# Fused attention and two MLP layers on one core: attention's instructions in an order computed in the source, fixed tiles, pair 0 loaded head by head

## The chip, the cores and the metric

The kernel runs on one core of a Trainium2 chip. The metric is device time in microseconds (us) of one execution, the median of the runs shown; lower is better. The core's engines run their own instruction queues in order: PE (TensorE, matmuls and transposes), DVE (VectorE), ACT (ScalarE), POOL (GpSimd) and SP (SyncE, which here only issues transfers).

## The reference

Attention with rotary embedding on q and k, then two MLP layers on the attention's output:

```python
q, k, v: (2, 8, 576, 64); tokens 2*576 = 1152; d_model 512; d_ff 1536 and 2048
q_rot, k_rot = rotate(q), rotate(k)
scores = matmul(q_rot, k_rot.T) / sqrt(64)
attn = exp(scores - max(scores)); attn = attn / (sum(attn) + 1e-9)
x = (attn @ v) as (1152, 512)
x = ((x @ w_a) * (x @ w_b)) @ w_out
h = x @ w_in;  out = (h - tanh(h)) @ w_out2
```

## The kernel before

**Precision.** Every operand of a real matmul is split into a high part (a rounded fp32r copy) and a low part (the remainder), so each product is made of two or three fp32r matmuls. A split costs a copy on ACT (the high part) and a subtraction on DVE or POOL (the low part). The weights come as 64-bit floats and are converted on ACT and DVE in pieces (`conv_unit`, L116) that are issued between other work.

**Attention by pairs of heads.** There are 2 batches with 8 heads: 8 pairs of heads, run one after the other as a software pipeline. For each pair:

- loads of q and k (`load_qk`, L237) and of v (`load_v`, L245), all on SP's queue; the rotary embedding (`rope_step`, L264), four instructions for q and four for k: on DVE for pair 1, on POOL from pair 2; the split of v (`prep_v`, L282: ACT, then POOL);
- `prep_T` (L342): PE transposes (L363), ACT makes the high part `th` (L366), DVE the low part (L368), and eight transfers on SP move them to `q2` and `k2` (L383);
- nine score units (`s_unit`, L387): 40 matmuls of 288 columns a pair (L409) into one of two score tiles in PSUM (tag `s`), the row maximum on DVE (L415), the exponential with the row sum on ACT (`s_exp`, L421). A score tile is free again after its exponential;
- the probabilities are transposed on PE (`t_unit`, L474; `t_tail`, L455, L460, L461: 42 transposes a pair) into three PSUM tiles of tag `t`, which `prep_T` and the normalization use too, and split by ACT (L479, L446) and DVE (L481, L448);
- `v_head` (L484): 40 matmuls (L501) into the accumulator; ACT copies it to `xe` (L523), a transfer moves one half to the other partitions of `xsum` (L525), and POOL adds the halves (L526). Pair 7 does this with ACT and DVE alone (L517, L519);
- `norm_sum` (L531) and `norm_pair` (L548): the reciprocal of the sums on DVE, spread by POOL into `rd` (L541, L545), transposed by PE (L554, L555: five), multiplied into `xsum` by DVE (L557, L560); then the output's high part by DVE (L562) and low part by POOL (L563).

Pair 0 is different: one transfer brings both heads of q or k per half of the partitions, and `rope_head` and `prep_head` (L299, L314) prepare it head by head on DVE, PE (L324) and ACT without transfers.

**What sets the order.** A loop over "slots" calls these functions at places that a table of offsets fixes (`at(...)`, L589 on; the offsets in `CFG`), and the framework's scheduler then reorders the instructions of each engine by its own estimates and by the priorities `P_...` in `CFG`. Tiles come from rotating pools. The result is a static order per engine. In the last pair the first pieces of weight conversion and the first matmuls of the next stage (`ab`, L190) are mixed in.

**After attention** come the matmuls of the two MLP layers (`ab`, `y`, `h`, `o`), with the weights' conversion between them. The change does not touch these functions.

Of the kernel before, what the change touches and what calls it, by code (L numbers as in the profile page):

```python
CFG = {'EXPF': 1, 'MAXF': 1, 'TT0': 20, 'TT1': 17.5, 'NS': 19, 'NP': 31, 'LK': -8, 'LQ': -2, 'RK': -2, 'RQ': 1, 'PK': 2, 'PQ': 4.5, 'LV': 7, 'PV': 9, 'WC1': 6, 'WC2': 4, 'PST': 3, 'RE': 2, 'FST': 0, 'CY': 1, 'CA': 2, 'CH': 2, 'OE': 3, 'VA0': 5.5, 'VA1': 7, 'VB0': 0, 'VB1': 2, 'PKD': 1, 'PQD': 0, 'PVD': 2, 'PVE': 0, 'XHE': 2, 'RST': 0, 'PA': 99, 'PB': 0, 'PO': 4, 'YLP': 4, 'GA': 0, 'GB': 0, 'WF': 99, 'WCE': 5, 'NH': 2, 'HA': 0, 'NT2': 2, 'RB': -50, 'SB': -49, 'NW': 20, 'NW1': 6, 'TM': 1, 'CO': 1, 'CHB': 0, 'WG': 99, 'WCG': 4, 'TL': 7, 'P_pl': 0, 'P_norm_sum': 30, 'P_load_v': 0, 'P_prep_v': 30, 'P_pT': 60, 'P_tl': -15, 'XL': 7, 'RDP': 1, 'P_ph': 0, 'P_exp': -60, 'P_V': 0, 'P_rope_head1': 0, 'P_load_qk': 15, 'P_S': 0, 'P_xs': -15, 'P_T': 0}
# [10 lines left out]
F32 = mybir.dt.float32  # L12
# [13 lines left out]
C2 = 0.052115944387372236  # L26


@with_exitstack
def attention_moe_kernel(  # L30
# [13 lines left out]
    nc = tc.nc  # L44
# [171 lines left out]
    with ExitStack() as actx:  # L216
        ap1 = actx.enter_context(tc.tile_pool(name="ap1", bufs=1))
        ap2 = actx.enter_context(tc.tile_pool(name="ap2", bufs=2))
        sctx = ExitStack()
        ps_s = sctx.enter_context(  # L220
            tc.tile_pool(name="ps_s", bufs=2, space=bass.MemoryType.PSUM, side="right")
        )
        ps_t = actx.enter_context(tc.tile_pool(name="ps_t", bufs=PST, space=bass.MemoryType.PSUM, side="left"))
        ps_v = actx.enter_context(tc.tile_pool(name="ps_v", bufs=4-PST, space=bass.MemoryType.PSUM, side="left"))

        rtab = ap1.tile([P, 2, 5 * D], F32, name="rtab")
        zero = ap1.tile([P, 2 * D], F32, name="zero")
        raw = [ap1.tile([P, 2, 5, D], F32, name=f"raw{n}") for n in "qk"]
        q2 = []
        for i in range(2):  # L230
            t = mid.tile([P, 2, 2, 640], F32R, tag="mid", name=f"q2{i}")
            q2.append(t)
        v2 = [ap1.tile([P, 10, 2 * D], F32R, name=f"v2{i}") for i in range(2)]

        def halves(t, b, hp):
            return t[b, 2 * hp:2 * hp + 2].rearrange("h (r c) d -> r h c d", c=CW)

        def load_qk(i, n):
            b, hp = PAIRS[i]
            s = halves((q, k)[n], b, hp)  # L240
            t = raw[n]
            nc.sync.dma_start(out=t[0:64], in_=s[:, :, 0:5])
            nc.sync.dma_start(out=t[64:128, :, 0:4], in_=s[:, :, 5:9])

        def load_v(i):  # L245
            b, hp = PAIRS[i]
            vr = ap1.tile([P, 2, CM, D], F32, tag="vr", name="vr")
            vt = ap1.tile([P, D], F32, tag="vt", name="vt")
            s = halves(v, b, hp)
            nc.sync.dma_start(out=vr[0:64], in_=s[:, :, 0:4])  # L250
            nc.sync.dma_start(out=vr[64:128], in_=s[:, :, 5:9])
            vf = v[b, 2 * hp:2 * hp + 2].rearrange("h (r c) d -> (h r) c d", c=CW)
            nc.sync.dma_start(out=vt, in_=vf[:, 4])
            vraw[i] = (vr, vt)

        vraw = {}
        k2 = {}
        pt = {}
        sums = {}
# [3 lines left out]
        rtmp = {}  # L263
        rot = {}  # L264

        def rope_step(n, step, eng):
            t = raw[n].rearrange("p h c d -> p c h d")
            if step == 0:
                rtmp[n] = ap1.tile([P, 5, 2, D], F32, tag=f"r2{n}", name="r2")
                rot[n] = ap1.tile([P, 5, 2, D], F32, tag=f"ro{n}", name="ro")  # L270
            if step < 2:
                o0, o1 = step * hd, (1 - step) * hd
                eng.tensor_tensor(
                    out=rtmp[n][:, :, :, o0:o0 + hd], in0=t[:, :, :, o1:o1 + hd],
                    in1=sb[:, :, :, o0:o0 + hd].to_broadcast([P, 5, 2, hd]), op=ALU.mult,
                )
            elif step == 2:
                eng.tensor_tensor(out=rot[n], in0=t, in1=cb.to_broadcast([P, 5, 2, D]), op=ALU.mult)
            else:
                eng.tensor_tensor(out=rot[n], in0=rot[n], in1=rtmp[n], op=ALU.add)  # L280

        def prep_v(i, h):  # L282
            vr, vt = vraw[i]
            v2i = v2[i % 2]
            cp = (nc.scalar.copy, nc.gpsimd.tensor_copy, nc.vector.tensor_copy)[PVE]
            if h < 2:
                dst = v2i[:, 4 * h:4 * h + 4, :]
                hi, lo = (dst[:, :, D * x:D * x + D] for x in (h, 1 - h))
                cp(out=hi, in_=vr[:, h])
                nc.gpsimd.tensor_tensor(out=lo, in0=vr[:, h], in1=hi, op=ALU.subtract)  # L290
                return
# [54 lines left out]
        def prep_T(i, n, h):  # L346
# [25 lines left out]
            if h == 0:  # L372
                return
# [531 lines left out]
```

## Time and profile before

| what | value |
|---|---|
| three runs | 625.51, 624.96, 621.99 us; median 624.96 us |
| the profiled execution | 619.34 us, its span 617.6 us |
| PE busy | 587.5 us (95% of the span) |
| DVE, ACT, POOL busy | 486.0 us (79%), 347.8 us (56%), 133.1 us (22%) |
| stretch of attention | from about 17 us (first score matmul) to about 192 us |

The profiled execution is 5.6 us below the median of the runs. The page gives busy times and what bounded the end; windows give busy time by stretch, the timeline single instructions with what they waited for, and the chain of waits the work that released each next step. Matmuls are pipelined, so that a busy PE is not yet a PE at its best rate.

### The profile page before, as it was taken

How to read it: one execution, taken by the hardware profiler on the slowest of the kernel's cores; microseconds unless marked ns; L12 is line 12 of the kernel's file. 1: busy time of each engine (PE TensorE's matmuls, PEld its weight loads, DVE VectorE, ACT ScalarE, POOL GpSimd, SP SyncE). 2: the span in 40 equal slices, each digit the busy share in tenths (PEclk: the TensorE clock that was granted, in tenths of full speed). 3: DMA queues.
4: the chain of work that ended last, by engine and by line, in shares of the span. 5: the costliest groups of instructions: out<-in, count | busy, mean ns of one | idle time of the engine just before them, and what ended most of it. 6: DMA issues, size and time to landing. Idle time of an engine off the chain costs nothing.

```text
span 617.6 us, 9091 instructions
## 1 busy us (share of the span) xinstructions
PE 587.5 (95%) x3468; PEld 551.8 (89%) x3468; DVE 486.0 (79%) x654; ACT 347.8 (56%) x579; POOL 133.1 (22%) x137
## 2 busy tenths in 40 slices
PE   7699998799989999999999999999999999999997
PEld 6588997788879999999999999989988988998975
DVE  7988888778888989787747468798976797899572
ACT  2588887688864566434223233358775773575350
POOL 2758888863320000000000000190000000000000
PEclk9999999999999999999999999999999999999999
DMA  4565765456243555424212123320001122300014
GB/s 118 144 155 138 187 153 142 125 137 140 79 146 109 187 183 174 167 70 136 69 59 78 69 69 137 119 86 1 1 24 45 69 69 68 115 22 1 1 41 112
DMA packets 37771, 60.91 MB, mean 99 GB/s; under 512 B 4064, under 2 KB 22496, under 8 KB 37728
## 3 DMA queue, kind: packets, MB, share of 16 engines
q1 hardware_dynamic: 37728, 60.34, 33.6%
q8 instruction: 27, 0.44, 0.3%
q14 instruction: 16, 0.13, 0.1%
HBM read 43.06 MB, written 2.36 MB: 74 GB/s over the span
## 4 chain that ended last, share of the span: by engine, by line
PE 72%; DVE 10%; ACT 8%; POOL 3%; DMA 3%; issue 2%; SPq 0%; POOLq 0%; ACTq 0%; DVEq 0%
PE ab L190 23%; PE h L190 11%; PE o L828 11%; PE y L190 9%; PE pss L409 5%; PE acc L501 5%; PE pst L474 4%; PE ow L828 3%; POOL yt L721 2%; ACT p L421 2%; ACT ph L479 2%; PE psp L363 1%; ACT st L127 1%; POOL xsum L526 1%; DMA st<-in_moe_w_in_dram 1%
## 5 line engine op out<-in xcount | busy, mean ns | idle before, releaser
L190 PE MATMUL ab<-xt,w 128*128 128x384 f32 x504 | 89.2, 335 | 1.3 <-DVE xsum L557 0.8
L190 PEld LDWEIGHTS ab<-xt,w 128*128 128x128 f32 x504 | 87.3, 188 | 1.8 <-issue 1.1
L828 PE MATMUL o<-wc,g 128*128 128x512 f32 x348 | 83.7, 392 | 0.5 <-ACT g L803 0.4
L828 PEld LDWEIGHTS o<-wc,g 128*128 128x128 f32 x348 | 64.7, 188 | 14.1 <-ACT g L803 1.4
L190 PE MATMUL y<-g,wc 128*128 128x384 f32 x432 | 76.5, 334 | 0.0
L190 PEld LDWEIGHTS y<-g,wc 128*128 128x128 f32 x432 | 75.0, 188 | 0.0
L409 PE MATMUL pss<-k,q 128*128 128x288 f32 x320 | 62.4, 315 | 6.6 <-ACT p L421 4.5
L190 PE MATMUL h<-yt,w 128*128 128x384 f32 x360 | 65.5, 335 | 0.0
L190 PEld LDWEIGHTS h<-yt,w 128*128 128x128 f32 x360 | 62.9, 188 | 1.7 <-issue 0.4
L190 PE MATMUL ab<-xt,wc 128*128 128x384 f32 x360 | 63.2, 334 | 0.0
L190 PEld LDWEIGHTS ab<-xt,wc 128*128 128x128 f32 x360 | 62.5, 188 | 0.0
L415 DVE TENSOR_REDUCE nm<-pss 128x1 f32<-128x576 f32 x72 | 53.5, 752 | 11.2 <-PE pss L409 10.9
L721 POOL TENSOR_TENSOR yt<-yacc,yt 128x384 fp32r<-128x384 f32 x12 | 17.6, 1497 | 206.1 <-ACT yt L720 206.1
L501 PE MATMUL acc<-ph,v 128*128 128x288 f32 x320 | 56.8, 307 | 3.5 <-ACT ph L479 2.6
L127 ACT ACTIVATE st<-st 128x1024 f32<-128x1024 f32 x34 | 39.8, 1170 | 35.4 <-DMA st<-in_moe_w_b_dram 16.4
L421 ACT ACTIVATE p<-pss,nm 128x576 f32<-128x576 f32 x72 | 54.1, 752 | 7.2 <-DVE nm L415 6.9
L409 PEld LDWEIGHTS pss<-k,q 128*128 128x128 f32 x320 | 45.8, 189 | 11.9 <-ACT p L421 9.0
L688 ACT COPY tmpa<-ab 128x384 f32<-128x384 f32 x36 | 17.2, 477 | 60.7 <-PE ab L190 60.6
L474 PE MATMUL pst<-ident,p 128*128 128x128 f32 x288 | 45.2, 274 | 5.6 <-DVE xsum L557 2.3
L481 DVE TENSOR_TENSOR ph<-pst,ph 128x512 fp32r<-128x512 f32 x72 | 48.2, 684 | 2.6 <-ACT ph L479 2.2
L501 PEld LDWEIGHTS acc<-ph,v 128*128 128x128 f32 x320 | 45.5, 188 | 5.3 <-ACT ph L479 1.6
L479 ACT CAST ph<-pst 128x512 fp32r<-128x512 f32 x72 | 42.0, 594 | 12.2 <-PE pst L474 11.4
(120 smaller groups left out, 984.6 us busy)
## 6 DMA issues: line engine op xcount, KB each, us to landing
st<-in_moe_w_out_dram SPq DMA_DIRECT2D x14, 1024.0 KB, 4.8
st<-in_moe_w_in_dram SPq DMA_DIRECT2D x8, 1024.0 KB, 5.1
q<-th SPq DMA_DIRECT2D x28, 288.0 KB, 5.1
st<-in_moe_w_a_dram SPq DMA_DIRECT2D x12, 512.0 KB, 3.6
st<-in_moe_w_b_dram SPq DMA_DIRECT2D x12, 512.0 KB, 4.8
k<-th SPq DMA_DIRECT2D x28, 160.0 KB, 2.7
vr<-in_v_dram SPq DMA_DIRECT2D x16, 128.0 KB, 2.9
out_dram<-oacc SPq DMA_DIRECT2D x16, 128.0 KB, 2.4
```

The lines of the kernel that those rows point to most:

```text
L127: nc.scalar.activation(out=xs.bitcast(F32), in_=xs.bitcast(F32), func=AF.Copy, scale=2.0 ** -112)
L190: nc.tensor.matmul(ps, w(a), x(c), start=start and n == 0, stop=stop and n == 2)
L409: nc.tensor.matmul(ph[:, a], st, k2[i][:, j, ko + a * HS:ko + (a + 1) * HS], start=(n == 0), stop=(n == len(mms) - 1),)
L415: nc.vector.tensor_reduce(out=nm[:, u:u + 1], in_=ph, axis=AX.XY, op=ALU.max, negate=True)
L421: nc.scalar.activation(out=po.rearrange("p (a x) -> p a x", a=2), in_=ph, func=AF.Exp, bias=nm, scale=1.0, accum_out=sm,)
L474: nc.tensor.transpose(ps[:, t * P:(t + 1) * P], p[:, t, o:o + P], ident)
L479: nc.scalar.copy(out=pu[:, 0, qm(i)], in_=ps)
L481: nc.vector.tensor_tensor(out=pu[:, 1, qm(i)], in0=ps, in1=pu[:, 0, qm(i)], op=ALU.subtract)
L501: nc.tensor.matmul(acc, st, pslot(i, u)[:, s, a * HS:(a + 1) * HS], start=(u == 8 and s == 0), stop=(u == full[-1] and s == 1),)
L688: nc.scalar.copy(out=a[:, t], in_=r[0])
L721: (nc.gpsimd if YLP > d else nc.vector).tensor_tensor(out=yl, in0=o, in1=yh, op=ALU.subtract)
L828: nc.tensor.matmul(ps, g[:, a, i * P:(i + 1) * P], wc[:, c, f % 2], start=(n == 0 and m == 0), stop=(n == GE - 1 and m == 2),)
```

## The change

- `make_ops` lists every instruction group of the attention (some 90 a pair) with its engine, its duration, what it reads and writes, and its PSUM tile. `plan` places them in time, engine by engine, by these durations and by a rank (`OFF`, one number per kind, found beforehand). The groups are emitted in the order of the planned starts, and up to the last exponential the framework keeps that order on all five queues (`tc.manual_schedule`). The rest of pairs 6 and 7 is emitted in the planned order too, with a piece of weight conversion each 1.3 us of planned time, and there the framework may still reorder. The priorities are gone.
- The tiles are fixed ones (two `k2`, two `p`, one `xe`, one `xsum`, and so on) in place of pools that rotate. The PSUM pools stay: three tiles of tag `t`, two of `s`, one accumulator.
- Pair 0's q and k come in eight transfers, one per head and half of the partitions: four issued by ACT at its start, four by SP; q's first head is prepared first.
- The embedding of pair 1 moves from DVE to POOL. The output's high part moves from DVE (L562) to ACT, its low part from POOL (L563) to DVE.

```diff
+def make_ops(NPR, XL):
...
+            op(i, f"S{u}", "PE", c * .132, (c - 1) * .132 + .33, r=kq, w=[g], g=g, args=(i, u))
+            op(i, f"max{u}", "DVE", .668, .76, r=[g], w=[("nm", b, u)], g=g, args=(i, u))
+            op(i, f"exp{u}", "ACT", .735, .76, r=[g, ("nm", b, u)], w=[pb + (u,), ("sm", b, u)], g=g, args=(i, u))
...
+        op(i, "xh", "ACT", .55, .65, r=xk, w=[("xh", i)], args=(i,))
+        op(i, "xl", "DVE", .67, .75, r=xk + [("xh", i)], w=[("xl", i)], args=(i,))
+    return ops
...
+def plan(ops, off, noise=None, look=0.0, start=None):
+    n = len(ops)
+    rank = [o[0] * II + off.get(o[1], 0.0) + off.get((o[1], o[7]), 0.0) for o in ops]
...
+START = {'DVE': 5.2, 'PE': 6.0, 'SP': 3.3, 'ACT': 3.0, 'POOL': 12.0}
+OFF = {
+    'S0': -25.13, 'S1': -41.8, 'S2': 6.72, 'S3': 0.3, 'S4': 4.19, 'S5': 10.11, 'S6': 14.05, 'S7': 8.11, 'S8': 2.6,
...
-                    eng = nc.vector if j < RE else nc.gpsimd
-                    at(g0 + LK, load_qk, j, 1)
-                    at(g0 + LQ, load_qk, j, 0)
...
-            (nc.scalar.copy, nc.gpsimd.tensor_copy, nc.vector.tensor_copy)[XHE](out=xh, in_=x)
-            nc.gpsimd.tensor_tensor(out=xl, in0=x, in1=xh, op=ALU.subtract)
...
+        def x_hi(_, i):
+            nc.scalar.copy(out=x_out(i)[0], in_=x)
+
+        def x_lo(_, i):
+            xh, xl = x_out(i)
+            nc.vector.tensor_tensor(out=xl, in0=x, in1=xh, op=ALU.subtract)
...
+        for j in range(2):
+            for n in (1, 0):
+                s = halves((q, k)[n], 0)
+                nc.scalar.dma_start(out=raw[n][0:64, j], in_=s[:, j, 0:5])
+                nc.sync.dma_start(out=raw[n][64:128, j, 0:4], in_=s[:, j, 5:9])
...
+        ops = make_ops(NPR, XL)
+        begin = plan(ops, OFF, start=START)[0]
+        todo = sorted(range(len(ops)), key=lambda n: begin[n])
+        scored = max(n for n, o in enumerate(todo) if ops[o][:2] in ([NPR - 1, f"exp{u}"] for u in range(9))) + 1
...
+        with tc.manual_schedule(engines=set(engines)):
+            for o in todo[:scored]:
+                emit[ops[o][1]](ops[o][6], *ops[o][7])
...
+        last = begin[todo[scored]]
+        for o in todo[scored:]:
+            while begin[o] > last + CVT:
+                cv(1)
+                last += CVT
+            emit[ops[o][1]](ops[o][6], *ops[o][7])
```

How the order moves, at three places. In the rows, `pss` is a score tile, `psp` the transposes of q or k, `pst` those of the probabilities, `acc` the accumulator, `ro` or `rot` the embedded q or k, `r` or `rtmp` its partial products.

PE in the fill of the pipeline, from the first score matmul of pair 0; before:

```order
L409 MATMUL pss<-k_145,q_93 128x288 x12
L363 MATMUL psp<-ident,ro 128x128 x6
L409 MATMUL pss<-k_145,q_93 128x288 x16
L363 MATMUL psp<-ident,ro 128x128 x6
L460 MATMUL pst<-ident,p_241 128x128
L461 MATMUL pst<-ident,p_241 64x128
L409 MATMUL pss<-k_145,q_93 128x288 x4
L474 MATMUL pst<-ident,p 128x128 x4
L409 MATMUL pss<-k_145,q_93 128x288 x4
L474 MATMUL pst<-ident,p 128x128 x8
L409 MATMUL pss<-k_145,q_93 128x288 x4
```

With the change:

```order
L649 MATMUL pss<-k_98,q_96 128x288 x8
L584 MATMUL pss<-ident,rotk 128x64
L584 MATMUL pss<-ident,rotk 128x128 x4
L767 MATMUL warm<-ident 128x128 x6
L649 MATMUL pss<-k_98,q_96 128x288 x20
L671 MATMUL pst_321<-ident,p_104 128x128 x4
L671 MATMUL pst_327<-ident,p_104 128x128 x4
L671 MATMUL pst_334<-ident,p_104 128x128 x4
L649 MATMUL pss<-k_98,q_96 128x288 x8
L541 MATMUL psp_357<-ident,rotq 128x128 x4
L541 MATMUL psp_366<-ident,rotq 128x128 x2
L649 MATMUL pss<-k_98,q_96 128x288 x4
```

Score matmuls now start before k's second head is transposed (`rotk` after the first eight), pair 0's scores and the transposes of its probabilities run on without the transposes of pair 1 between them (`psp` came after 12 score matmuls, now after 36 and 12 transposes).

POOL around the end of a pair in the middle of the attention (`xsum<-xe` adds the halves, `rd<-rs` spreads the reciprocals, `v` is the split of v); before:

```order
L526 TENSOR_TENSOR xsum<-xe,xsum 64x576
L541 COPY rd<-rs 128x512
L545 COPY rd<-rs 128x128
L526 TENSOR_TENSOR xsum<-xe,xsum 64x576
L273 TENSOR_TENSOR r_1497<-rawk,rtab 128x10x32 x2
L273 TENSOR_TENSOR r_1585<-rawq,rtab 128x10x32
L278 TENSOR_TENSOR ro<-rawk,rtab 128x640
L563 TENSOR_TENSOR xt_73<-xsum,xt_72 128x576
L280 TENSOR_TENSOR ro<-ro,r_1497 128x640
L273 TENSOR_TENSOR r_1585<-rawq,rtab 128x10x32
L278 TENSOR_TENSOR ro<-rawq,rtab 128x640
L280 TENSOR_TENSOR ro<-ro,r_1585 128x640
```

With the change:

```order
L736 COPY rd<-rs_112 128x512
L740 COPY rd<-rs_112 128x128
L635 TENSOR_TENSOR v_100<-vr,v_100 128x4x64
L533 TENSOR_TENSOR rotq<-rotq,rtmpq 128x640
L526 TENSOR_TENSOR rtmpk<-rawk,rtab 128x10x32 x2
L526 TENSOR_TENSOR rtmpq<-rawq,rtab 128x10x32
L719 TENSOR_TENSOR xsum<-xe,xsum 64x576
L635 TENSOR_TENSOR v_100<-vr,v_100 128x4x64
L719 TENSOR_TENSOR xsum<-xe,xsum 64x576
L635 TENSOR_TENSOR v_100<-vt,v_100 64x64 x2
L526 TENSOR_TENSOR rtmpq<-rawq,rtab 128x10x32
```

The two additions stood on either side of the spreading; now both come behind it, with parts of later pairs' embedding and of v between them, and the output's low part (`xt`) is gone from POOL.

DVE at the same place (`nm` is the row maximum, `xsum<-xsum` the normalization, `xt` the output); before:

```order
L415 TENSOR_REDUCE nm<-pss 128x1 x2
L560 TENSOR_TENSOR xsum<-xsum,rt 64x64
L557 TENSOR_TENSOR xsum<-xsum,rb 128x512
L560 TENSOR_TENSOR xsum<-xsum,rt 64x64
L415 TENSOR_REDUCE nm<-pss 128x1
L562 CAST xt_72<-xsum 128x576
L368 SCALAR_TENSOR_TENSOR th<-psp,th 128x448
L481 TENSOR_TENSOR ph<-pst,ph 128x512
L368 SCALAR_TENSOR_TENSOR th<-psp,th 128x192
L415 TENSOR_REDUCE nm<-pss 128x1
```

With the change:

```order
L678 TENSOR_TENSOR ph_116<-pst_1619,ph_116 128x512
L655 TENSOR_REDUCE nm_109<-pss 128x1
L747 TENSOR_TENSOR xsum<-xsum,psrb 128x512
L751 TENSOR_TENSOR xsum<-xsum,psrt 64x64 x2
L655 TENSOR_REDUCE nm_109<-pss 128x1
L678 TENSOR_TENSOR ph_115<-pst_1663,ph_115 128x512
L655 TENSOR_REDUCE nm_108<-pss 128x1
L678 TENSOR_TENSOR ph_115<-pst_1683,ph_115 128x512
L762 TENSOR_TENSOR xt_73<-xsum,xt_72 128x576
L655 TENSOR_REDUCE nm_108<-pss 128x1
```

The output's cast, which followed one maximum after the normalization, is replaced by the low part's subtraction, which stands two maxima and two splits (`ph`) behind the normalization.

## Rows read from the trace of the kernel before

**Rows 1.** The page, part 2: the granted TensorE clock in 40 slices.

```profile
PEclk9999999999999999999999999999999999999999
```

**Rows 2.** Windows: stretch, length, busy us (instructions) of PE, PEld, DVE, ACT, POOL; clock; DMA.

```profile
17.11:35.74 18.63, 13.32 (x88) 10.22 (x86) 17.47 (x30) 13.24 (x35) 15.52 (x16) 1.00 0.64 160
35.74:168.81 133.07, 122.48 (x926) 114.70 (x926) 110.04 (x203) 107.86 (x278) 91.22 (x95) 1.00 0.56 138
55.00:115.00 60.00, 54.99 (x424) 52.03 (x422) 50.56 (x97) 49.85 (x129) 52.14 (x54) 1.00 0.64 157
55.00:155.00 100.00, 90.31 (x693) 85.07 (x691) 82.44 (x156) 80.91 (x210) 74.27 (x78) 1.00 0.60 145
168.81:191.80 22.99, 20.16 (x136) 18.40 (x135) 21.07 (x35) 12.50 (x23) 3.69 (x4) 1.00 0.42 137
```

**Rows 3.** Timeline of PE: start us, us, line, op, out<-in, count [idle before <-releaser].

```profile
17.11 0.38 PE L409 MATMUL pss<-k,q 128*128 128x288 f32 x1
...
35.74 0.51 PE L409 MATMUL pss<-k,q 128*128 128x288 f32 x2
...
54.95 0.38 PE L554 MATMUL rb<-ident,rd 128*128 128x128 f32 x2
...
155.10 0.38 PE L554 MATMUL rb<-ident,rd 128*128 128x128 f32 x2
```

**Rows 4.** Chain of waits, stretches of PE alone: start us, us, what.

```profile
66.90 1.32 PE acc L501 x10
...
68.66 0.53 PE pss L409 x4
69.20 0.44 PE pst L474 x4
...
191.80 8.21 PE ab L190 x46
```

**Rows 5.** Waits of PE, 55 to 155 us: total us, times, longest.

```profile
PE pst L474 <- DVE xsum L557: 2.3, 2, 1.3
PE pst L474 <- DVE th L368: 1.6, 2, 1.0
...
PE psp L363 <- DVE xsum L560: 0.7, 1, 0.7
```

**Rows 6.** Chain of waits at one end of a pair.

```profile
112.75 1.35 POOL xsum L526
...
116.79 1.44 POOL xsum L526
...
118.25 0.69 DVE xsum L557
...
120.02 1.78 DVE xt L562
```

**Rows 7.** Timeline of DVE at the start.

```profile
2.27 0.20 DVE L580 CAST q<-zero 128x64 fp32r<-128x64 f32 x1 [0.75 <-ACT zero L575]
...
6.17 0.56 DVE L304 TENSOR_TENSOR r<-rawk,rtab 128x160 f32<-128x160 f32 x2 [2.06 <-DMA rawk<-in_k_dram]
```

**Rows 8.** Chain of waits in pair 0's scores.

```profile
23.70 0.68 DVE nm L415
...
24.40 0.84 ACT p L421 x2
```

**Rows 9.** Timeline of DVE, two instructions of one form beside POOL and without it.

```profile
8.26 1.02 DVE L308 TENSOR_TENSOR r<-rawq,rtab 128x320 f32<-128x320 f32 x1
...
11.19 0.48 DVE L308 TENSOR_TENSOR r<-rawk,rtab 128x320 f32<-128x320 f32 x1
```

**Rows 10.** One line's instructions: duration ns min/median/max, first and last start.

```profile
L562 DVE CAST xt<-xsum x8: 450/460/1785, 59.7 to 191.7; 128x576 fp32r<-128x576 f32 x8
```

**Rows 11.** Waits of SP's queue, 55 to 155 us.

```profile
SPq L525 <- ACT xe L523: 14.4, 3, 10.4
```

**Rows 12.** The page, part 6: transfers, count, KB each, median us to landing.

```profile
q<-th SPq DMA_DIRECT2D x28, 288.0 KB, 5.1
```

More of the change, by code (lines that the diff above doesn't have):

```diff
@@ L235, in halves @@
[L235 to L254, printed above, removed]
@@ new lines, in v_hi, with v_lo, s_ph, s_mm @@
+        def v_hi(_, i, h, j):
+            dst, src = v_part(i, h, j, 0)
+            nc.scalar.copy(out=dst, in_=src)
+        def v_lo(_, i, h, j):
+            dst, src = v_part(i, h, j, 1)
+            nc.gpsimd.tensor_tensor(out=dst, in0=src, in1=v_part(i, h, j, 0)[0], op=ALU.subtract)
+        def s_ph(g):
+            return tile_of(g).rearrange("p (a x) -> p a x", a=2)[:, :, 0:HS]
+        def s_mm(g, i, u):
+            mms = []
+            for j in ((0, 1) if u == 8 else (u // 4,)):
+                for s in range(2):
+                    o, ko = (SM * (1 - j), 64) if u == 8 else ((u % 4 + j) * P, 64 * (1 - j))
+                    mms.append((q2[i % 2][:, s, j, o:o + P], j, ko))
+            for m, (st, j, ko) in enumerate(mms):
+                for a in range(2):
+                    nc.tensor.matmul(
+                        s_ph(g)[:, a], st, k2[i % 2][:, j, ko + a * HS:ko + (a + 1) * HS],
+                        start=(m == 0), stop=(m == len(mms) - 1),
+                    )
@@ new lines, in t_mm, with t_hi, t_lo, tail_T @@
+        def t_mm(g, i, u):
+            o = SM if u == 8 else u * P + (u // 4) * P
+            for t in range(CM):
+                nc.tensor.transpose(tile_of(g)[:, t * P:(t + 1) * P], pt[i % 2][:, t, o:o + P], ident)
+        def t_hi(g, i, u):
+            nc.scalar.copy(out=pslot(i, u)[:, 0, qm(i)], in_=tile_of(g))
+        def t_lo(g, i, u):
+            dst = pslot(i, u)
+            nc.vector.tensor_tensor(out=dst[:, 1, qm(i)], in0=tile_of(g), in1=dst[:, 0, qm(i)], op=ALU.subtract)
+        def tail_T(g, i, part):
+            t, p = tile_of(g), p8[i % 2]
@@ new lines, in v_mm, with x_copy, x_move @@
+        def v_mm(g, i, j, a, u, first, last):
+            st = v2[i % 2][:, 8 + j if u == 8 else u, :]
+            for s in range(2):
+                nc.tensor.matmul(
+                    tile_of(g), st, pslot(i, u)[:, s, a * HS:(a + 1) * HS],
+                    start=first and s == 0, stop=last and s == 1,
+                )
+        def x_copy(g, i, j, a):
+            nc.scalar.copy(out=xe[:, j, a * HS:(a + 1) * HS], in_=tile_of(g))
+        def x_move(_, i, j):
+            nc.sync.dma_start(out=x[half(j)], in_=xe[half(1 - j), j])
```

796 lines of the change are left out of this document (423 added, 373 removed), and 14 rows, old and new, of the table OFF.

## Prediction

> **What bounds the kernel now.** I first read the clock: the granted TensorE clock is 9 tenths or more in all 40 slices [rows 1], so 2.4 GHz throughout, and no stretch is slow for that reason. Then I read the windows. From 192 us to the end the MLP layers keep PE nearly full, and the change leaves them alone, so the question is what happens from 17 to 192 us. There the busy times show no clear bound: over three pairs (55 to 115 us) PE is busy for 55.0 us of 60, POOL 52.1, DVE 50.6, ACT 49.9 [rows 2]. Four engines are at 83 to 92% and none is full, which is what an order that lets them wait for each other looks like.
>
> The timeline gives the rate. The normalization's transposes `rb` of one pair start at 54.95 us and those of the fifth pair after it at 155.10 [rows 3]: 20.03 us a pair. What PE needs for a pair is found from pieces of the chain in which PE waits for nothing: 10 matmuls of 288 columns in 1.32 us, 4 in 0.53, 4 transposes in 0.44 [rows 4], so 0.132 and 0.11 us each. A pair has 40 score matmuls, 40 of the accumulator and 59 transposes (42 of probabilities, 12 of q and k, 5 of the normalization): 80 x 0.132 + 59 x 0.11 = 17.05 us. **So 3.0 us of every 20 are lost to waiting**, and PE's work is the floor.
>
> Where it waits: in 55 to 155 us PE is idle for 100 - 90.31 = 9.7 us [rows 2], and 4.6 of these end with DVE's normalization or DVE's split of q and k just behind it [rows 5] (the rest of the loss is pipeline refill after each stop: busy 90.3 against 85.3 of work). The chain at one such place shows the cause [rows 6]: POOL adds the halves of `xsum` (1.35 us, then 1.44 behind the spreading), DVE's normalization can only follow (0.69), then the output's cast takes 1.78 us in DVE's queue, and PE's next transposes wait behind all that.
>
> **The ledger.** Up to the 42nd `ab` matmul both orders give PE the same work (320 score and 320 accumulator matmuls, 524 transposes), so the change in time is the change in waiting. I cut at three marks: first score matmul of pair 0, first of pair 1, last of pair 7.
>
> Before: 17.11 to 35.74 us [rows 3], 18.63 us for 40 score matmuls and 44 transposes (10.1 us of work), 8.5 us of waiting; 35.74 to 168.81 us, 133.07 us [rows 2] for 280 + 270 matmuls and 374 transposes (113.7), 19.3 of waiting, which is 2.76 for each of 7 pairs; 168.81 to 191.80 us, 22.99 us for 50 matmuls, 42 transposes and 42 `ab` matmuls (18.7, with `ab` at 8.21 / 46 = 0.178 us [rows 4]), 4.3 of waiting.
>
> **The change part by part.**
>
> *Start.* The first embedding step on DVE waits for a transfer until 6.17 us [rows 7]. Smaller transfers on two queues should land sooner, but ACT now issues four of them before the instruction that DVE's clearing casts wait for; those began at 2.27 us [rows 7] and will begin some 2 us later. I count nothing for the start itself (bounds: 1.5 us sooner, 0.5 later). The first score matmul now needs only the first head of k and q: half an embedding and one split fewer in front of it on DVE, and no instruction of pair 1, which was in between. I take 15.5 us in place of 17.11 (13.5 to 17.1).
>
> *Fill.* With two score tiles, each held for a score unit (0.53), a maximum (0.68) and an exponential (0.84) [rows 4, 8] and the hand-overs, a unit takes at least 1.1 us, and with the splits that share DVE and ACT some 1.5: nine units need about 13 us, so the last exponential of pair 0 falls at about 29. Five more transposed units and the splits follow, and pair 1's first score matmul comes at about **32.5 us** (30.5 to 35.7, the upper end being today's mark). Pair 1's embedding is now on POOL instead of DVE; it is hidden there, because POOL has nothing else to do then; if that cover is gone, pair 1 waits until the upper end. By that mark PE has done 40 + 12 matmuls and 65 transposes (14.0 us).
>
> *Middle.* To the last score matmul there are 280 + 248 matmuls and 358 transposes: 109.1 us. The waiting is the term that decides. It can fall to about 0.3 us a pair (a fully interlocked order) or stay at 2.76. The new order takes the chain at the pair's end apart: both additions come long before the normalization, since 10 us of PE work stand between a pair's last accumulator matmul and its `rb`, against some 6 us for copy, transfer and two additions. So the 4.6 of 9.7 us go; of the rest I let half go, since it consists of single waits that a list with measured durations also sees. 2.76 x 2.55 / 9.7 = 0.7 us. What is late next: POOL has 52.1 / 3 = 17.4 us of work in a pair and loses the low part (1.4, as long as an addition of the same 576 columns [rows 6]): 16.0. ACT has 49.9 / 3 = 16.6 and gets the high part, between the cast's 0.45 [rows 10] and an exponential of the same length, 0.84 [rows 8]: some 17.2. DVE has 50.6 / 3 = 16.9, loses the cast's 0.45 and gets a subtraction like the normalization's 0.69 [rows 6]: 17.1. All three are within about 1 us of PE's 17.05, so any slip meets a full queue. And the new subtraction on DVE meets POOL. In the start one DVE instruction with both inputs in SBUF took 1.02 us beside POOL and 0.48 with POOL idle [rows 9]; the cast that is removed took 0.45 at best and 1.79 at worst [rows 10]. I add 0.4 for this and take **1.2 us a pair**, 8.4 in all (bounds 2.1 and 19.3).
>
> The Trainium skill ("SBUF — State Buffer", section "Who interferes with whom") says that a DVE instruction with two SBUF inputs and a POOL instruction that reads SBUF exclude each other: the later one waits out the other whole. Rows 9 agree for the embedding; by the rule taken strictly the new subtraction would wait in nearly every pair, which is the first rival below.
>
> *Drain.* Left are 60 matmuls, 48 transposes and 42 `ab` matmuls: 20.7 us. The waiting was 4.3; the last subtraction now stands on DVE between pieces of weight conversion instead of on POOL, which was idle there (3.7 us busy of 23 [rows 2]). I add 1.0 (one conversion piece): 5.3 (4.3 to 9).
>
> **Sum.** 32.5 + 109.1 + 8.4 + 20.7 + 5.3 = 176.0 us for the mark at 191.8: 15.8 us sooner. The profiled execution took 619.34 us (span 617.6), so 603.5 by it; it lies 5.6 below the median of the runs, and against that median the forecast is 624.96 - 15.8 = **609.2 us**, 2.5% faster.
>
> **The rivals.**
>
> 1. *DVE and POOL hold each other, and the rate stays.* If the subtraction waits out a POOL instruction of 1.5 us in each pair, and POOL, at 16 of 17 us, loses 0.7 more, the queues are full at about 19 to 20 us a pair. Then waiting stays at 2.76: 32.5 + 109.1 + 19.3 + 26.0 = 186.9, 4.9 us sooner: 620.0. For it: rows 9 and 10. Against it: in five pairs of before the cast was rarely hit (median 460 ns). Chance 0.12.
> 2. *PE becomes the bound.* The order holds and waiting falls to 0.3 a pair: 169.7, so 22.1 us sooner: 602.9. For it: the pieces of [rows 4], where PE already runs at its rate. Against it: three more engines with 16 to 17 us each. Chance 0.18.
> 3. *Slower: SP's queue.* The order on SP is fixed too. SP stood up to 10.4 us in front of a move of `xe` [rows 11]; a transfer of q lands 5.1 us after its issue [rows 12]. Where such a move stands ahead of the next pair's q and k and its accumulator is late, the next scores wait, and with them everything in the fixed order. At 5.1 us a pair on top of 1.2: 32.5 + 109.1 + 44.1 + 26.0 = 211.7, 19.9 later: 644.9. It decides from 2.7 us a pair on (waiting 3.9 a pair gives today's time plus 0.5%). Against it: the transfers were off the chain in most pairs. Chance 0.06.
>
> That the change does nothing is excluded by the printed orders, which differ on all queues.
>
> **How the numbers follow.** The forecast has the remaining 0.64. A difference of 0.5% (3.1 us) is what a measurement of this kernel can tell from none: faster means under 621.8. The forecast's own range is 600 (all good bounds but the rate's: 30.5, 0.3 to 0.5 a pair) to 619 (waiting 2 us a pair, drain 7, fill 34 to 35). Rival 2 lies inside, rival 1 at its upper edge: 599 to 620 leaves out rival 3, half of rival 1 and the tails of the forecast. Faster: 0.64 + 0.18 + half of rival 1 = 0.87 (with a little of the forecast's tail taken off); same 0.07; slower 0.06.
>
> **What would show it.** Right: `rb` about 18.2 us apart in the middle; pair 1's first score matmul near 32.5 us; DVE's normalization no longer waits for POOL's `xsum`; the span from the 42nd `ab` matmul on unchanged to 1 us. Wrong: `rb` still 20 us apart with the subtraction at 1.5 us or more (rival 1); PE waits for transfers of `q` or `k` (rival 3); or a gain in the middle that the drain gives back in waits for converted weights.

## The result, and the profile after

The changed kernel takes 615.38 us (median of 4 runs, 615.03 to 616.49), the kernel before beside it 625.24 (4 runs, 621.99 to 626.09): a ratio of 0.9855, 95% interval [0.9817, 0.9892], so 1.5% faster. Forecast were 609.2 us and a range of 599 to 620.

The profiled execution took 616.49 us. Its page, busy times and granted clock:

```profile
span 614.7 us, 9129 instructions
...
PE 586.5 (95%) x3468; PEld 556.6 (91%) x3468; DVE 482.9 (79%) x646; ACT 351.8 (57%) x587; POOL 130.7 (21%) x137
...
PEclk8699999999989999999999999999999999999999
```

Against [rows 1] the clock is below 9 tenths in slices 1, 2 and 12. The windows below lie between the marks of the prediction, with one from 55 to 155 us, and answer to [rows 2]; the columns are as there:

```profile
16.59:40.86 24.27, 20.08 (x117) 17.90 (x118) 16.18 (x28) 15.55 (x39) 16.75 (x20) 0.79 0.44 111
40.86:159.41 118.55, 112.08 (x886) 109.29 (x886) 107.20 (x195) 106.70 (x275) 83.99 (x90) 1.00 0.68 161
55.00:155.00 100.00, 95.81 (x763) 93.88 (x764) 90.88 (x170) 91.33 (x235) 71.57 (x77) 1.00 0.68 161
159.41:188.30 28.89, 25.03 (x152) 22.80 (x151) 26.38 (x43) 16.10 (x30) 4.16 (x4) 0.88 0.37 121
```

The same cuts as a ledger, with two kernels of the experiments (e3: the low part on POOL in pairs 6 and 7; e8: fewer conversion pieces in the drain); us, with the granted clock of the fill and the drain where it is under 0.97:

| stretch | before | forecast | the change | e3 | e8 |
|---|---|---|---|---|---|
| start, to the first score matmul | 17.11 | 15.5 | 16.59 | 16.50 | 16.50 |
| fill, to pair 1's first score matmul | 18.63 | 17.0 | 24.27 (0.79) | 21.28 | 21.26 |
| middle, to pair 7's last | 133.07 | 117.5 | 118.55 | 117.96 | 116.43 |
| drain, to the 42nd `ab` | 22.99 | 26.0 | 28.89 (0.88) | 27.36 (0.94) | 23.31 |
| the rest | 425.8 | 425.8 | 426.4 | 429.1 | 430.1 |
| span | 617.6 | 601.8 | 614.7 | 612.2 | 607.6 |

The middle came as forecast. PE's timeline shows the normalization's transposes of one pair and those of the fourth pair after it; they are 17.94 us a pair apart (20.03 in [rows 3], forecast 18.2):

```profile
85.81 0.38 PE L744 MATMUL psrb<-ident,rd 128*128 128x128 f32 x2
...
157.55 0.60 PE L744 MATMUL psrb<-ident,rd 128*128 128x128 f32 x4
```

PE's waits from 55 to 155 us no longer name DVE's normalization, which led [rows 5]:

```profile
PE pss L649 <- DMA k<-thk: 1.7, 2, 1.0
PE pss L649 <- ACT ph L697: 1.3, 1, 1.3
PE pss L649 <- DMA q<-thq: 1.3, 1, 1.3
PE pss L649 <- ACT xt L758: 1.0, 2, 0.6
```

The loss is at both ends. In the fill PE's timeline shows the second head of k behind a score tile that an exponential frees, and the clock is at its lower level soon after PE's stop:

```profile
16.59 1.32 PE L649 MATMUL pss<-k,q 128*128 128x288 f32 x8 [2.33 <-DVE k L603]
19.53 1.41 PE L584 MATMUL pss<-ident,rotk 64*128 64x64 f32 x5 [1.63 <-ACT p L659]
```

```profile
18.50:28.70 10.20, 8.41 (x35) 7.93 (x36) 4.33 (x7) 5.54 (x15) 7.07 (x8) 0.53 0.32 90
180.00:186.00 6.00, 5.18 (x19) 5.18 (x20) 3.81 (x10) 2.23 (x3) 0.00 (x0) 0.50 0.49 167
```

These two windows of the change have a granted clock of 0.53 and 0.50, that is 1.2 GHz for nearly all of them. The second is in the drain, where PE had stopped for 2.0 and 0.8 us:

```profile
179.21 0.79 PE L424 MATMUL ab<-xt,w 128*128 128x384 f32 x2 [2.02 <-DVE xt L762]
180.82 2.77 PE L707 MATMUL acc<-ph,v 128*128 128x288 f32 x10 [0.83 <-DVE xsum L726]
```

### The profile page after: what moved, and what is told of

Its sections match the earlier page's. It is cut to its first block, busy times and chain, and to the rows that moved or that the text cites. A ratio compares the mean times of both kernels' runs of the same rounds, so it can differ in the third digit from the quotient of the medians.

```text
span 614.7 us, 9129 instructions
## 1 busy us (share of the span) xinstructions
PE 586.5 (95%) x3468; PEld 556.6 (91%) x3468; DVE 482.9 (79%) x646; ACT 351.8 (57%) x587; POOL 130.7 (21%) x137
## 4 chain that ended last, share of the span: by engine, by line
PE 70%; DVE 10%; DMA 8%; ACT 6%; POOL 3%; issue 1%; POOLq 0%; SPq 0%; ACTq 0%; DVEq 0%
PE ab L424 24%; PE o L990 11%; PE h L424 10%; PE y L424 9%; PE pss L649 4%; PE acc L707 4%; PE ow L990 3%; POOL yt L883 3%; PE pst L671 2%; DMA st<-in_moe_w_out_dram 2%; ACT p L659 1%; DMA k<-thk 1%; DVE nm L655 1%; DVE ph L678 1%; PE psp L541 1%
## 5 line engine op out<-in xcount | busy, mean ns | idle before, releaser
L424 PE MATMUL ab<-xt,w 128*128 128x384 f32 x504 | 91.0, 339 | 2.5 <-DVE xt L762 2.0
L424 PEld LDWEIGHTS ab<-xt,w 128*128 128x128 f32 x504 | 88.7, 191 | 3.1 <-DVE xt L762 2.3
L649 PE MATMUL pss<-k,q 128*128 128x288 f32 x320 | 59.2, 316 | 9.3 <-DVE k L603 2.3
L707 PE MATMUL acc<-ph,v 128*128 128x288 f32 x320 | 58.1, 310 | 1.0 <-DVE xsum L726 0.8
L649 PEld LDWEIGHTS pss<-k,q 128*128 128x128 f32 x320 | 47.2, 197 | 11.8 <-ACT p L659 3.7
L365 DVE SCALAR_TENSOR_TENSOR st<-st 128x1024 int32<-128x1024 int32 x34 | 43.1, 1267 | 4.5 <-ACT st L361 3.6
L369 DVE SCALAR_TENSOR_TENSOR st<-st 128x1024 int32<-128x1024 int32 x34 | 43.2, 1272 | 0.4
```

The lines of the kernel that those rows point to most:

```text
L365: (pe if PO & 1 else nc.vector).scalar_tensor_tensor(out=w, in0=xs, scalar=3, in1=w, op0=ALU.logical_shift_left, op1=ALU.bitwise_or)
L369: (pe if PO & 2 else nc.vector).scalar_tensor_tensor(out=w, in0=xs, scalar=SIGN_BIT, in1=w, op0=ALU.bitwise_and, op1=ALU.bitwise_or)
L424: nc.tensor.matmul(ps, w(a), x(c), start=start and n == 0, stop=stop and n == 2)
L649: nc.tensor.matmul(s_ph(g)[:, a], st, k2[i % 2][:, j, ko + a * HS:ko + (a + 1) * HS], start=(m == 0), stop=(m == len(mms) - 1),)
L707: nc.tensor.matmul(tile_of(g), st, pslot(i, u)[:, s, a * HS:(a + 1) * HS], start=first and s == 0, stop=last and s == 1,)
```

## The experiments

All are edits of the changed kernel. Ratios are to runs of the kernel before on the same chip; the changed kernel itself was not run again beside them.

| kernel | median us (runs) | ratio [95%] |
|---|---|---|
| e1, table load on a tile of its own | 613.87 (6) | 0.9841 [0.9803, 0.9878] |
| e2, filler transposes in the fill | 618.18 (6) | 0.9884 [0.9841, 0.9928] |
| e3, low part on POOL in pairs 6, 7 | 615.69 (6) | 0.9875 [0.9834, 0.9915] |
| e4, order left to the framework | 638.62 (6) | 1.0220 [1.0182, 1.0257] |
| e5, low part on POOL in all pairs | 614.20 (4) | 0.9869 [0.9828, 0.9910] |
| e6, pair 0 by four transfers | 615.42 (6) | 0.9880 [0.9841, 0.9919] |
| e7, another order in the start | 615.05 (6) | 0.9878 [0.9849, 0.9906] |
| e8, fewer pieces in the drain | 609.65 (6) | 0.9771 [0.9729, 0.9814] |
| e9, e7 + e2 + e5 | 613.52 (6) | 0.9814 [0.9771, 0.9856] |
| e10, e9 + fillers in the drain | 616.66 (6) | 0.9859 [0.9815, 0.9902] |
| e11, e8 + e1 | 609.64 (6) | 0.9737 [0.9701, 0.9773] |

**e4: is it the fixed order?**

```diff
-        with tc.manual_schedule(engines=set(engines)):
+        with nullcontext():
```

> The change with one edit: the groups are emitted in the same planned order, but the framework may reorder them on every engine during the whole attention, by its own estimates, as before the change. Theory D (the fixed order is what shortens the pair): the normalization's transposes of successive pairs stand 19 to 20 us apart again instead of 17.9, and the total is 8 to 14 us above the change, as slow as before or slower. Rival (what shortened the pair is the fixed tiles and the work moved between DVE, ACT and POOL, or the emission order alone): the pairs stay at 18 to 18.5 us and the total within 3 us of the change.

The kernel becomes 23 us slower than the change and 2.2% slower than before. Cut at the marks of the ledger, its profile (span 634.3 us against 614.7) loses 6.9 us in the start, with the first score matmul at 23.46, and 12.9 in the middle, which takes 131.4 us (118.55 in the change); the fill, the drain and the rest differ by 0.5 at most. The middle's clock was 0.97, so a part of the 12.9 may be the clock's. The normalization's transposes come at uneven distances of 16.9 to 25.2 us, 21.0 on average (17.94 in the change), and PE waits longest for the accumulator's copy (45 to 170 us):

```profile
PE acc L707 <- ACT xe L713: 4.5, 5, 2.2
```

That is theory D: within the changed kernel the fixed order makes the rate, and without it the middle is about as long as before (133.07). The fixed tiles and the emission order alone are worse in total than before, by more than was expected. Here the framework had no priorities, unlike in the kernel before; the fixed order on rotating tiles, and the fixed tiles under the old priorities, were not tested.

**e5: is it the balance of DVE and POOL?**

```diff
-            nc.vector.tensor_tensor(out=xl, in0=x, in1=xh, op=ALU.subtract)
+            nc.gpsimd.tensor_tensor(out=xl, in0=x, in1=xh, op=ALU.subtract)
```

> The change with the low part of the output on POOL for every pair, as before, in the same emitted order: DVE loses 0.75 us a pair, POOL gets 1.45. Theory A (POOL, at about 16 of 18 us, is as near the limit as DVE, so moving the subtraction to DVE was needed for the rate): the normalization's transposes come 18.5 to 19.5 us apart in place of 17.94, and the median is 620 to 626. Theory B (the fixed order alone makes the rate; the balance between DVE and POOL doesn't matter): 17.8 to 18.1 us apart, and the median stays within 2 us of the change's 615.4.

This is theory B. The middle takes 117.89 us against 118.55, the transposes are 18.1 us apart, and the median is 614.20. The rows give one line's instructions (duration min/median/max ns), of the change and then of e5:

```profile
L762 DVE TENSOR_TENSOR xt<-xsum,xt x8: 747/750/1671, 71.1 to 187.1; 128x576 fp32r<-128x576 f32 x8
```

```profile
L762 POOL TENSOR_TENSOR xt<-xsum,xt x8: 1424/1438/1814, 68.4 to 182.7; 128x576 fp32r<-128x576 f32 x8
```

On DVE the subtraction was held up once in eight (1671 ns against 750), so rival 1, with a hit in nearly every pair, does not occur, and moving it to DVE was not needed either. The timelines of DVE and POOL say why it was rare: the slow one began at 71.07 us, while a POOL instruction ran (70.56 to 72.13); behind one other a POOL instruction began in its last 0.2 us; during the remaining six POOL stood idle.

**e1, e6, e7: is the start late, and does it matter?**

```diff
-        nc.scalar.activation(out=zero[:, 0:1], in_=zero[:, 0:1], func=AF.Square)
+        nc.scalar.activation(out=tabl, in_=zero[:, 0:1], func=AF.Square)
```

> The change with one edit: the activation that loads ACT's table at the start writes a tile of its own, so that DVE's twelve clearing casts no longer wait for ACT, which issues four transfers first. In the change they began at 4.88 us and the first embedding step at 6.65. Theory A (the fill is late because DVE starts late): first embedding step at about 5.4 us (when q's first head lands), first score matmul at 15.3 instead of 16.59, pair 1's first at 39.5 instead of 40.86, total 1.2 us below the change. Theory B (the fill is late because PE's stops let the granted clock fall to half): the stretch at half clock from 19.5 to 28.7 us stays as long, pair 1's first score matmul moves by the same 1.2 us or less; both agree on this run within a microsecond, which prices the start by itself. Rival: the transfers land no earlier than 6.3 us and nothing moves.

DVE's embedding begins at 5.64 us in place of 6.65, but the first score matmul comes at 16.82 (expected: 15.3). The two rows below are of one form on DVE. The first took 0.48 us; the second took 1.82 beside POOL's embedding of pair 1, and the split of k stood behind it. So the transfers land early enough (the rival is refuted), but the start's saving does not come.

```profile
6.12 0.48 DVE L574 TENSOR_TENSOR rtmpq<-rawq,rtab 128x320 f32<-128x320 f32 x1
...
14.15 1.82 DVE L574 TENSOR_TENSOR rtmpk<-rawk,rtab 128x320 f32<-128x320 f32 x1
```

e6 undoes the loading head by head:

```diff
...
-                nc.scalar.dma_start(out=raw[n][0:64, j], in_=s[:, j, 0:5])
-                nc.sync.dma_start(out=raw[n][64:128, j, 0:4], in_=s[:, j, 5:9])
...
+            nc.sync.dma_start(out=raw[n][0:64], in_=s[:, :, 0:5])
+            nc.sync.dma_start(out=raw[n][64:128, :, 0:4], in_=s[:, :, 5:9])
```

> The change with pair 0's q and k loaded by four transfers of two heads each, all issued by SP as before, and none by ACT. Theory A (the loading head by head costs: ACT's four issues hold back the instruction that DVE's clearing casts wait for): the casts begin near 2.3 us in place of 4.9, the embedding near 6.2 in place of 6.65, the first score matmul comes some 0.4 us sooner than 16.5, and the median lies 0 to 1 us below the change's. Theory B (smaller transfers land sooner, and that is worth more than the issues cost): the embedding begins later than 6.65 and the median lies above the change's.

The clearing casts begin at 2.27 us again, the embedding at 6.43 (6.65), yet the first score matmul is later (17.38), at a clock of 0.73 up to there, and the median is the change's. Neither theory is shown: this part is worth nothing that could be measured. e7 takes e1's tile and moves pair 0's splits, and with them the load of pair 1's v, in the emitted order:

```diff
...
+        late = [o for o in todo if ops[o][:2] in ([0, "vlo"], [1, "loadv"])]
+        todo = [o for o in todo if o not in late]
+        n = todo.index(find(1, "rope0", (0, 2))) + 1
+        todo[n:n] = late
+        o = find(0, "hl10")
+        todo.remove(o)
+        todo.insert(todo.index(find(0, "hrope11", (1, 1, 2))), o)
```

> As e1 (the table-loading activation writes a tile of its own, so that DVE starts at about 5.6 us), and in the emitted order two moves for pair 0: POOL's split of v goes behind three instructions of pair 1's embedding, away from DVE's embedding, and DVE's split of the first head of k goes ahead of the last products of k's second head. Theory A (the start is late because DVE's queue stands beside POOL and holds the split of k behind work that is not yet needed): the first score matmul comes at 15.2 us or before (16.8 in e1, 16.6 in the change), pair 1's first score matmul 1 to 1.5 us sooner than in e1 at the same granted clock, and the median 1 to 1.5 us below e1's 613.9. Theory B (in the fill the two score tiles set the rate, whatever comes first): the first score matmul comes at 15.2 us too, but pair 1's first score matmul moves by less than 0.5 us, and the median stays at 613.9.

The first score matmul comes at 15.14 us, as both theories said. Pair 1's first comes at 38.50 and the median is 615.05, which speaks for theory B. The clock was 0.91 in that fill, so the 38.50 cannot be set straight against e3's 37.78; e9 below compares at full clock. The earlier start is lost because DVE takes the first two maxima only at 17.37 us (17.77 in e3), when the rest of k's embedding is done.

**e2, e3: what does the clock cost in the fill?** e2 puts eight filler transposes, which nobody reads, behind each of the first five score units, and 34 in place of 20 at the start (`NW`, not in the cut):

```diff
...
+            nsc[0] += 1
+            if nsc[0] <= 5:
+                warm(8)
```

> The change with more transposes of the identity that nobody reads: 34 instead of 20 at the start and 8 behind each of pair 0's first five score units, to keep PE busy in its stops. Theory B (half clock): the granted clock stays at 1.0 from 8 to 30 us, score units of 8 matmuls take 1.3 us instead of 2.27 there, and pair 1's first score matmul comes 3 to 4 us sooner (about 37.3 instead of 40.86); total 3 to 4 us below the change. Theory A (late start and the chain score, maximum, exponential, free tile): the clock is high but pair 1's first score matmul moves by less than 1 us, since DVE and ACT set the pace, or comes up to 1 us later because of the added transposes.

e3 gives the low part of the last two pairs back to POOL:

```diff
-            nc.vector.tensor_tensor(out=xl, in0=x, in1=xh, op=ALU.subtract)
+            eng = nc.gpsimd if i >= 6 else nc.vector
+            eng.tensor_tensor(out=xl, in0=x, in1=xh, op=ALU.subtract)
```

> The change with one edit: the output's low part of pairs 6 and 7 is made by POOL, which is idle there, as it was before the change; in the change it stands on DVE behind three pieces of weight conversion, and PE waited 2.0 us for pair 6's and then ran at half clock from 180 to 186 us. Theory C (the drain loses to DVE's queue): PE's wait for pair 6's low part falls from 2.0 to under 0.7 us, the accumulator's last ten matmuls start 2 us sooner, the clock stays up, and the total is 2 to 4 us below the change. Rival (the drain is bound by DVE's conversion as a whole, so freeing 1.5 us on it only moves the wait to the weights or to the halves' addition): less than 1 us.

In e2 the clock stays at 1.00 through the fill and pair 1's first score matmul comes at 38.41 us: 2.5 sooner than in the change, but 0.6 later than in e3, which has no such fillers. The median is no better, with runs near 613 and near 618, so neither theory is met in full. e3 leaves the fill alone. Its window, to be read beside the change's first one above:

```profile
16.50:37.78 21.28, 16.78 (x118) 14.06 (x118) 15.98 (x28) 15.36 (x39) 16.83 (x20) 1.00 0.51 126
```

These are the same instructions at full clock: 21.28 us against 24.27, and e8, whose fill is the same too, took 21.26 at 1.00. So 3.0 us of the change's fill are the clock of that execution, and the other 4.3 above the forecast are not. In the drain PE's wait for pair 6's low part fell only from 2.0 to 1.5 us (expected: under 0.7), because a piece of conversion still stands inside the normalization on DVE; e3 saved 1.5 us there, and its median shows nothing of it.

**e8: the drain.**

The number is the planned time from one piece of weight conversion to the next:

```diff
...
-'CVT': 1.3}
+'CVT': 2.0}
```

> The change with a piece of weight conversion each 2.0 us of planned time instead of 1.3 in the drain, nothing else. Theory A (in the drain PE waits because pair 6's and pair 7's last steps on DVE stand behind conversion pieces): PE's wait for pair 6's low part falls from 2.0 us to under 1, the 42nd `ab` matmul comes 1 to 2 us sooner after the last score matmul (28.5 us in the change), and the median lies 1 to 2 us below the change's 615.4. Theory B (the pieces have to be done in any case, and the `ab` matmuls wait for them later): the wait for the low part shrinks too, but waits for converted weights take its place before or behind the 42nd `ab` matmul, and the median stays at 615 to 617.

This is theory A, but more than its 1 to 2 us: the median is 609.65 us, and each of its runs is below the change's lowest. The drain takes 23.31 us in place of 28.89, at full clock:

```profile
154.19:177.50 23.31, 22.18 (x152) 20.28 (x151) 22.76 (x39) 14.82 (x29) 4.13 (x5) 1.00 0.43 144
```

That difference is not one of single executions: the drain is 28.5 to 29.2 us in all five profiles that leave it alone (the change, e1, e2, e6, e7), with 2.0 us of waiting for pair 6's low part in each, and 23.3 and 23.4 in the two with the new number (e8, e11). The rows show DVE's queue, first of the change, then of e8 (L362, L365, L369 and L388 are conversion pieces, L762 the low part of pair 6, L726 pair 7's addition of halves):

```profile
176.12 1.23 DVE L365 SCALAR_TENSOR_TENSOR st<-st 128x1024 int32<-128x1024 int32 x1
177.26 1.22 DVE L388 TENSOR_TENSOR w<-st,w 128x1024 fp32r<-128x1024 f32 x1
178.40 0.75 DVE L762 TENSOR_TENSOR xt<-xsum,xt 128x576 fp32r<-128x576 f32 x1
179.07 1.22 DVE L369 SCALAR_TENSOR_TENSOR st<-st 128x1024 int32<-128x1024 int32 x1
180.32 1.30 DVE L726 TENSOR_TENSOR xsum<-acc,xe 64x288 f32<-64x288 f32 x3
```

```profile
168.98 1.23 DVE L369 SCALAR_TENSOR_TENSOR st<-st 128x1024 int32<-128x1024 int32 x1
170.24 0.76 DVE L762 TENSOR_TENSOR xt<-xsum,xt 128x576 fp32r<-128x576 f32 x1
170.92 0.69 DVE L362 TENSOR_SCALAR st<-st 128x1024 int32<-128x1024 int32 x1
171.64 0.81 DVE L726 TENSOR_TENSOR xsum<-acc,xe 64x288 f32<-64x288 f32 x2
```

In the change three pieces of 1.2 us stand before the low part (the two shown, and one at 173.72 us inside the normalization) and a fourth before the addition; PE waits behind each of these two steps and then runs at half clock. In e8 one piece of 1.2 us is left before the low part and a short one before the addition, PE's longest stop there is 0.47 us, and the clock stays. No wait for weights takes its place: the `ab` matmuls run on without a stop. Of the 7.1 us between the two profiles only the drain's 5.6 belong to this edit; the fill's 3.0 are the clock, and the rest took 3.7 longer, as it did by 2.7 in e3 with the change's pieces.

**e9, e10, e11: what adds up.** e9 joins e7, e2 and e5 without further edits.

> The parts that each looked useful, together: the start of e7 (own tile for the table-loading activation, k's split ahead, v's split behind), the filler transposes of e2 in the fill, and the low part of the output on POOL as in e5. Theory A (start, granted clock in the fill and drain are separate losses, and their savings add up): first score matmul at 15.2 us, full clock through the fill, pair 1's first score matmul at 36 to 37.5 us, the middle 117 us long, and the median 610 to 612. Theory B (PE's stops come from the two score tiles and the fillers only take their place, so that an earlier start is lost in the fill): pair 1's first score matmul at 38 us or later and the median at 613 to 615.

The median is 613.52 us, and theory B holds: the first score matmul comes at 14.35 us and pair 1's first at 38.25, against 15.81 and 38.41 in e2, both at full clock. The middle took 121.68 us: once PE waited 1.95 us for a transfer of k, the clock was 0.92 from 119.80 to 140.50 us, and four score matmuls behind the wait took 1.07 us (0.77 in e8). That is not all of it: e10's middle, the same instructions, took 119.99 us at full clock, 2 to 3 us more than with the parts alone (117.89 in e5, 117.35 in e7, 117.26 in e2); why is not shown.

```profile
123.94 1.07 PE L652 MATMUL pss<-k,q 128*128 128x288 f32 x4 [1.95 <-DMA k<-thk]
```

e10 is e9 with fillers in the drain:

```diff
...
+            if ops[o][0] == NPR - 1 and ops[o][1] in ("xs", "rb"):
+                warm(6)
```

> As e9, and six filler transposes on PE after each of pair 7's additions and behind its normalization's transposes (30 in all, 3.3 us at full clock). Theory A (part of the drain is lost because the granted clock falls after PE's stops there): the clock stays above 0.95 from 170 to 190 us, the matmuls behind the stops run at full rate, and the median is 0.5 to 1.5 us below e9's. Theory B (the fillers stand in front of matmuls that were ready, or the clock falls all the same): the median lies 0 to 2 us above e9's.

This is theory B, the fillers in front of ready matmuls. e9's drain was at full clock without them, so there was no clock to save; it took 25.37 us, e10's 27.30. PE's busy time in it grew by 3.4 us, and only 1.5 of that came out of its idle time.

> e8 (a piece of weight conversion each 2.0 us of planned time) and e1's own tile for the table-loading activation, which starts DVE 1.0 us sooner; nothing else. Theory A (start and drain are separate losses, and an earlier start is kept): pair 1's first score matmul comes 0.5 to 1 us sooner than e8's 37.76 at full clock, and the median is 608 to 609.3 against e8's 609.65. Theory B (an earlier start is lost, because DVE's embedding then stands beside POOL for longer and the score tiles set the rate behind it): pair 1's first score matmul at 37.5 us or later at full clock, and the median at 609.3 to 611.

The median is 609.64 us, as e8's, so no gain of the earlier start can be seen. Pair 1's first score matmul came at 37.89, but the clock was 0.92 in that fill, so the profile does not decide between the theories, which were stated for full clock. e8 beats both kernels with one number changed.

**The kernel before, once more.**

> The kernel before, unchanged, for a second profiled execution: the first took 619.3 us, while its runs lie at 621 to 628. Theory A (the granted clock falls in some executions of the kernel before too): this profile, if it is 622 us or more, shows a stretch of half clock in the start, the fill or the drain that the first has not. Theory B (the extra time is spread or lies elsewhere): the clock is as in the first profile, and the marks of the start, the middle and the drain, or the MLP layers, take longer at the same clock.

This execution took 625.34 us, and theory A holds for the start and the fill. The rows give its page and three windows (the start, the fill, and a place between the MLP layers), and last the first profile of before at that place.

```profile
PEclk8799999999999999999999999998999999999999
```

```profile
0.00:19.58 19.58, 13.76 (x65) 12.00 (x65) 14.45 (x40) 5.82 (x13) 4.63 (x12) 0.75 0.40 107
19.58:38.66 19.08, 13.83 (x87) 11.63 (x85) 17.77 (x28) 12.04 (x33) 14.21 (x14) 0.90 0.65 158
415.20:425.20 10.00, 7.54 (x34) 6.58 (x33) 7.48 (x5) 4.76 (x6) 6.54 (x5) 0.87 0.10 41
```

```profile
411.80:421.80 10.00, 8.23 (x46) 7.52 (x45) 8.01 (x8) 5.88 (x7) 5.51 (x4) 1.00 0.19 74
```

Its first score matmul is 2.5 us later than in the first profile, the fill and the middle 0.45 each, the rest behind the 42nd `ab` 2.6 (428.4 against 425.8): together the 6.0 us of difference. Of the start's 2.5 us, 0.5 are a first transfer that landed later (embedding from 6.64 us, 6.17 in [rows 7]). So the profiled execution of before was one of its better ones; the 48 runs of before beside the result and the experiments took 619.8 to 628.6.

## Why the prediction was right, and where it was not

- **The rate: right.** Waiting in the middle was put at 1.2 us a pair; it is (118.55 - 109.1) / 7 = 1.35, in e8 1.05. (The working's 0.7 + 0.4 is 1.1 and not 1.2.) The chain of [rows 6] is gone: DVE's normalization waited for POOL's addition three times before, 4.3 us in all, and never in the change. e4 shows that the rate comes from the fixed order.
- **Rivals.** Rival 1 did not occur, by the durations of L762 and by e5. What it had wrong is not that DVE and POOL hold each other, which the one hit shows again, but how often the planned order lets this subtraction meet POOL. Rival 2 wanted 0.3 us a pair, which no kernel reached. Rival 3's mechanism is there in small: waits for transfers of k and q are 3.0 of PE's waits from 55 to 155 us, about 0.5 us a pair; a single one, in e9, took 1.95 us.
- **Fill: the step that failed.** "A unit takes at least 1.1 us, and with the splits that share DVE and ACT some 1.5: nine units need about 13 us". At full clock (e3) the chain of waits runs from the first score matmul at 16.50 us to the end of the last exponential at 33.07, so 1.84 us a unit, through maximum, exponential and score matmuls by turns; k's second head is a tenth user of the two score tiles, and its path alone takes four hand-overs:

```profile
18.56 0.84 ACT p L659 x2
19.45 0.87 PE pss L584 x5
20.34 0.66 ACT k L598
21.03 0.76 DVE k L603
21.82 0.77 DVE nm L655
```

  From that last exponential to pair 1's first score matmul it was 4.7 us, where some 3.5 were forecast. The waiting in the fill was put at 3.0 us; it is 21.28 - 14.0 = 7.3 at full clock and 10.3 in the change's profile.
- **Start: the sign was right, the gain a third.** ACT's four issues moved the casts to 4.88 us (2.27 in [rows 7]); this was counted at nothing, and the embedding began at 6.65, 0.5 us later than before and 1.0 later than in e1, which has no such wait. Then DVE ran beside POOL: the split of v on POOL took 3.90 us for two instructions against 1.43 later with the same shapes. The Trainium skill ("SBUF — State Buffer", section "Who interferes with whom") has DVE, with two inputs in SBUF, contend with a POOL instruction that reads SBUF. The start agrees, and so does the middle, where the one subtraction of eight that began while POOL ran took 1.67 us and the others 0.75.

```profile
8.90 3.90 POOL L635 TENSOR_TENSOR v<-vr,v 128x256 fp32r<-128x256 f32 x2 [7.60 <-ACT v L631]
```

```profile
27.99 1.43 POOL L635 TENSOR_TENSOR v<-vr,v 128x256 fp32r<-128x256 f32 x2
```

- **Drain: right sign, too small.** "One conversion piece", 1.0 us, was added to 4.3; the waiting is 28.89 - 20.7 = 8.2, inside the bounds (4.3 to 9). What stood there was four pieces instead of one, and the lower clock behind PE's stops.
- **The clock.** "So 2.4 GHz throughout" went by [rows 1]. The durations contradict it for the start of that profile: six filler transposes, the same each time, took 1.49 us at 9.28 (and again at 12.09), where [rows 1] has 9 tenths or more, and 0.82 at 14.82. In the second profile of before six took 1.48 us at 15.82, at a clock of 0.50. No term of the sum hangs on it, since the start's waiting was not counted; but that the clock would fall in some executions, in the fill and the drain, was no part of the prediction.

```profile
9.28 1.49 PE L568 MATMUL warm<-ident 128*128 128x128 f32 x6
...
14.82 0.82 PE L568 MATMUL warm<-ident 128*128 128x128 f32 x6
```

- **The sum.** By the profiles the change lies 12.9 us above the forecast (614.7 against 601.8): 1.1 start, 7.3 fill, 1.0 middle, 2.9 drain, 0.6 rest. The median lies only 6.2 above, mostly because the forecast was set against the median of before, 5.6 us above its profile; one further execution shows clock losses in that difference. That these errors offset each other is luck.

## What to carry to other kernels

A fixed order from measured durations pays in the steady state (here 2.1 us a pair), but the same list says little of the ends, where queues are filled with other work: look there for long pieces ahead of a short instruction that PE waits for, and space them first (here one number, 5.7 us by the medians). Cut the profile at the same marks in both kernels before explaining a total, and take a second profile of the kernel before when its profiled execution lies at the edge of its runs.

## What the runs showed of the hardware

The granted clock is not a property of the code alone. The same instructions of the fill ran at 1.00 in one execution and at 0.79 in another, 3.0 us apart. Between the MLP layers, where PE stops, the clock was 1.00 in the change and 0.79, then 0.87, over 20 us in e8, whose rest took 430.1 us against 426.4 (the first row is of the change, the others of e8 from the same place on):

```profile
408.30:418.30 10.00, 8.32 (x47) 7.68 (x46) 8.01 (x8) 5.99 (x7) 5.40 (x4) 1.00 0.17 68
```

```profile
397.50:407.50 10.00, 7.44 (x32) 6.49 (x31) 7.50 (x5) 4.37 (x6) 6.56 (x5) 0.79 0.10 39
407.50:417.50 10.00, 10.00 (x52) 10.00 (x51) 5.84 (x5) 7.12 (x7) 0.00 (x0) 0.87 0.00 0
```

The Trainium skill ("TensorE: Matmul & The Clock Gate", section "Part 1: The HAM clock gate") says that idleness takes the clock to its lower level and that where it comes back differs from run to run of one kernel. The traces agree: by the durations of its transposes PE last ran at half rate in the start up to 12.2 us in the change, 13.7 in e3 and 19.5 in the second profile of before, and the later stretches at the lower level follow stops of PE, in the fill, the drain and between the layers. What decides whether a given stop costs the clock stays open.

The clock column can miss a stretch at the lower level, as in the start of the first profile of before; the durations of one form of instruction are the surer sign. The clock also limits what the medians can tell: differences of 1 to 2 us between e1, e3, e5, e6 and e7 are not settled.
